# Carrying a small product to its places by transfers, and moving two normalizations to other engines

## The chip, the cores and the metric

The kernel runs on one core of a Trainium2 chip. The metric is the device time of one execution in microseconds (us); lower is better. A core has five engines that run side by side, each with its own queue of instructions that is worked off strictly in order: TensorE (PE in the profile; its weight loads are PEld), VectorE (DVE), ScalarE (ACT), GpSimd (POOL) and SyncE (SP), which here issues the transfers (DMAs) and computes nothing. An instruction that has to wait for a semaphore holds up everything behind it in its engine's queue. TensorE writes its products to PSUM, which VectorE and ScalarE can read and GpSimd can't; everything else lies in SBUF, 128 partitions wide.

## The reference

An attention over a memory of 32 slots for each of 8 batches with 8 heads, followed by a mixture of four expert networks over the 4608 rows that it gives:

```python
a = softmax(phi, axis=seq)                      # per batch, head, memory slot; 576 x 32
k_m = einsum('bhsm,bhsd->bhmd', a, k)           # 32 x 64 per head
v_m = einsum('bhsm,bhsd->bhmd', a, v)
scores = (q @ k_m.T) / sqrt(64)                 # 576 x 32 per head
attn = softmax(scores, axis=-1)
x = (attn @ v_m)  ->  4608 x 512                # all heads side by side
p = domain_probs / sum(domain_probs)
out = sum over e of p[:, e] * (relu(x @ w1[e]) @ w2[e])   # w1 512 x 1024, w2 1024 x 512
```

All inputs and the output are float32.

## The kernel before, in words

**Precision.** TensorE multiplies numbers of a shorter form (F32R). So a float32 operand is split in two parts: ScalarE writes a rounded copy (the high part), and VectorE or GpSimd subtracts it from the original (the remainder, the low part). A product then takes three matmuls: high by high, high by low, low by high. `split` (line 146) does this for a stretch of w1 or w2: line 147 is the copy, line 148 the subtraction.

**The main loop.** The product x @ w1 is never formed through x. Since x = attn @ v_m, the kernel multiplies v_m by w1 once per pair of batches and expert (called vw), and then attn by vw. There are 512 steps, 128 for each of four pairs of batches (`PAIR`), 32 for each expert, 8 for each half of a batch; a step stands for 128 of the 1024 hidden columns and 256 or 320 rows. `steps` (line 838) does four things for step s: `accumulate` of a finished group; `run_plan(s)`; `first(s + 2)`, the product attn @ vw with the relu (lines 554 to 556 on TensorE, line 566 the relu as high part on ScalarE, line 568 its remainder on VectorE); and `second(s)`, the product with w2 (lines 584 to 586). So the relu and the remainder of a step have two steps' time before `second` needs them.

**The plan.** Everything else is put into `plan`, a table written by hand of what is emitted in which step: loads and splits of w1 and w2, the attention of batches 1 to 7, the products vw. For batches 2 to 7 the table `ATT` gives the first step, the step of the write (`written`), the steps of the three score products and of the three transposes. The program is in that order on each engine from step 36 on (`manual_schedule`), and so is the part ahead of step 0, a sequence for batch 0 written out by hand. In steps 0 to 35 a scheduler may move instructions.

**Attention of a batch b that starts at step s.** `load_phi` at s; `phi_max` at s + 3; `phi_exp` at s + 4; `phi_norm` (line 209) at s + 5 and s + 6 for the two halves g: add a small number to the sum, take the reciprocal, multiply phi by it (line 213), and copy its last 64 columns behind it (line 214). Then come transposes on TensorE (line 228) and the products with k and v (line 283), into `v` and `kT` (`kv_pick`, line 306). `scores_mm` multiplies q by k_m, and one step later each, `scores_max` (VectorE), `scores_exp` (ScalarE, line 411) and `soft` follow; the last one ends in a product of the exponentials with the reciprocal of their sum (line 421). `transposes` (line 442) turns the result for `first`.

**Where v_m goes.** `v` of a batch lies on 128 partitions by 4 by 32. Two layouts are made of it. `vts[k]` (line 102) holds both batches of pair k with heads in the slots that `TURN` gives, high and low part side by side; `vw_mm` (line 459) multiplies it by w1, and `vw_out` (line 478) splits the product, a copy by ScalarE (line 482) and a subtraction by VectorE (line 483) for each of the batches asked for. It is written for batches 0 to 3 (`write_vt`). `vs` holds four batches, the high part on the first 64 partitions and the remainder on the other 64; `four` (line 501) multiplies it by w1 for four batches at once, and `to_memory` and `load_vw` take the results through HBM. It is written for all batches (`write_vs`): batches 0 to 3 are first read in step 72, batches 4 to 7 in step 232.

Before, `v_hi` (line 340) makes the high part `vh` on ScalarE (line 347); `write_vt` (line 350) brings the parts to their places by operations on 64 partitions, copies by VectorE where the place lies in the other half of the partitions (line 363), or by ScalarE where it doesn't (line 360), and subtractions by VectorE (line 364); `write_vs` (line 366) does the same with ScalarE (line 376) and VectorE (lines 378, 379). The steps `written` are 48 and 65 for batches 2 and 3, and 163, 181, 195 and 216 for batches 4 to 7; `write_vs` stands one step later.

**Loads.** SyncE issues all transfers. `take` (line 137) hands out a load and issues loads ahead, each of which waits for its stage buffer to be free.

## Time and profile before

| | |
|---|---|
| median of 3 runs | 1428.37 us (1424.88 to 1428.73) |
| profiled execution, whole | 1426.93 us |
| its span, first to last instruction | 1425.1 us |
| granted TensorE clock, mean over the span | 0.995 |
| TensorE busy | 1397.7 us |
| VectorE busy | 663.7 us |
| ScalarE busy | 568.3 us |
| GpSimd busy | 396.0 us |

The profile is of one execution. Its views: busy time of each engine, for the whole span or for stretches of it (a stretch's row gives its length, then for each engine the busy time and in brackets the count of instructions, then the granted clock, the share of time in which the DMA engines were busy, and GB/s); groups of instructions by line and shape (busy time, mean ns of one, and the idle time of the engine just before them with what ended it); waits (who waited for whom: total us, times, longest); the chain of waits that ended last; the timeline (start, length, engine, line, operation, what is written <- what is read, shapes, count, and in square brackets the idle time before it with what ended it); and transfers by line (KB each, median us from issue to landing). Line 12 of the kernel is L12. SPq and ACTq mark what an engine's queue itself does, such as issuing a transfer.

### The profile page before, as it was taken

How to read it: one execution, taken by the hardware profiler on the slowest of the kernel's cores; microseconds unless marked ns; L12 is line 12 of the kernel's file. 1: busy time of each engine (PE TensorE's matmuls, PEld its weight loads, DVE VectorE, ACT ScalarE, POOL GpSimd, SP SyncE). 2: the span in 40 equal slices, each digit the busy share in tenths (PEclk: the TensorE clock that was granted, in tenths of full speed). 3: DMA queues.
4: the chain of work that ended last, by engine and by line, in shares of the span. 5: the costliest groups of instructions: out<-in, count | busy, mean ns of one | idle time of the engine just before them, and what ended most of it. 6: DMA issues, size and time to landing. Idle time of an engine off the chain costs nothing.

```text
span 1425.1 us, 21643 instructions
## 1 busy us (share of the span) xinstructions
PE 1397.7 (98%) x7742; PEld 1218.4 (85%) x7742; DVE 663.7 (47%) x1562; ACT 568.3 (40%) x1524; POOL 396.0 (28%) x316
## 2 busy tenths in 40 slices
PE   7999999999999989999999999999999999999998
PEld 6888888888888878888888888888888888888887
DVE  7986556435553476464343345434343322223222
ACT  7655445433344445453353443534332312122221
POOL 4300244322234244342242433424220202020200
PEclk9999999999999999999999999999999999999999
DMA  6532322585232233245368676786841633233201
GB/s 235 177 106 89 106 94 83 195 251 154 75 122 86 70 130 99 75 134 138 104 234 265 231 265 185 260 229 213 256 141 45 186 75 103 75 104 75 60 30 37
DMA packets 62843, 199.16 MB, mean 140 GB/s; under 512 B 10384, under 2 KB 11536, under 8 KB 62736
## 3 DMA queue, kind: packets, MB, share of 16 engines
q1 hardware_dynamic: 62736, 197.77, 44.0%
q8 instruction: 62, 1.02, 0.3%
q14 instruction: 45, 0.37, 0.1%
HBM read 146.35 MB, written 51.38 MB: 139 GB/s over the span
## 4 chain that ended last, share of the span: by engine, by line
PE 90%; DVE 6%; ACT 2%; issue 1%; DMA 1%; SPq 0%; ACTq 0%; DVEq 0%
PE p L586 18%; PE p L584 17%; PE p L585 17%; PE p L554 9%; PE p L555 9%; PE p L556 9%; PE pv L507 3%; PE sc L392 2%; PE x L283 2%; DVE vw L483 1%; ACT vw L482 1%; PE pv L462 1%; PE pv L464 1%; PE pv L463 1%; DVE vt L364 1%
## 5 line engine op out<-in xcount | busy, mean ns | idle before, releaser
L148 POOL TENSOR_TENSOR w<-stage,w 128x512 fp32r<-128x512 f32 x230 | 297.5, 1297 | 752.7 <-ACT w L147 727.8
L568 DVE SCALAR_TENSOR_TENSOR h<-p,h 128x256 fp32r<-128x256 f32 x512 | 215.2, 421 | 427.0 <-ACT h L566 289.4
L586 PE MATMUL p<-w,h 128*128 128x512 f32 x1024 | 403.1, 394 | 5.6 <-DVE h L568 4.9
L584 PE MATMUL p<-w,h 128*128 128x512 f32 x1024 | 403.7, 394 | 0.0
L585 PE MATMUL p<-w,h 128*128 128x512 f32 x1024 | 403.1, 394 | 0.0
L566 ACT ACTIVATE h<-p 128x256 fp32r<-128x256 f32 x512 | 196.4, 384 | 488.6 <-PE p L556 471.2
L554 PE MATMUL p<-AT,vw 128*128 128x256 f32 (+1 forms) x1024 | 309.1, 302 | 1.9 <-DVE vw L483 1.8
L555 PE MATMUL p<-AT,vw 128*128 128x256 f32 (+1 forms) x1024 | 302.7, 296 | 0.3 <-DVE AT L454 0.3
L556 PE MATMUL p<-AT,vw 128*128 128x256 f32 (+1 forms) x1024 | 301.6, 295 | 0.1
L586 PEld LDWEIGHTS p<-w,h 128*128 128x128 f32 x1024 | 192.8, 188 | 50.4 <-DVE h L568 5.8
L554 PEld LDWEIGHTS p<-AT,vw 128*128 128x128 f32 x1024 | 193.1, 189 | 23.1 <-PE pv L464 2.5
L584 PEld LDWEIGHTS p<-w,h 128*128 128x128 f32 x1024 | 192.7, 188 | 23.3 <-ACT h L566 0.2
L585 PEld LDWEIGHTS p<-w,h 128*128 128x128 f32 x1024 | 192.9, 188 | 22.1
L555 PEld LDWEIGHTS p<-AT,vw 128*128 128x128 f32 x1024 | 193.9, 189 | 20.1 <-DVE AT L454 0.5
L556 PEld LDWEIGHTS p<-AT,vw 128*128 128x128 f32 x1024 | 192.8, 188 | 0.8 <-DVE vw L483 0.7
L147 ACT CAST w<-stage 128x512 fp32r<-128x512 f32 x264 | 162.1, 618 | 5.1 <-DMA stage<-in_w 2.8
L568 DVE SCALAR_TENSOR_TENSOR hm<-p,hm 128x64 fp32r<-128x64 f32 x256 | 56.0, 219 | 148.4 <-ACT h L566 146.8
L566 ACT ACTIVATE hm<-p 128x64 fp32r<-128x64 f32 x256 | 57.1, 223 | 160.4 <-PE p L556 160.4
L510 DVE TENSOR_TENSOR vst<-pv,vst 128x512 fp32r<-128x512 f32 x80 | 55.3, 692 | 113.1 <-ACT vst L509 112.8
L272 POOL TENSOR_TENSOR kvs<-stage,kvs 128x512 fp32r<-128x512 f32 x58 | 74.4, 1302 | 107.4 <-ACT kvs L271 106.5
L509 ACT CAST vst<-pv 128x512 fp32r<-128x512 f32 x80 | 47.0, 587 | 123.4 <-PE pv L507 123.4
L483 DVE TENSOR_TENSOR vw<-pv,vw 64x512 fp32r<-64x512 f32 x96 | 65.7, 687 | 29.8 <-ACT vw L482 28.1
(89 smaller groups left out, 1174.6 us busy)
## 6 DMA issues: line engine op xcount, KB each, us to landing
stage<-in_w SPq DMA_DIRECT2D x92, 512.0 KB, 4.0
vwd<-vst SPq DMA_DIRECT2D x80, 512.0 KB, 3.5
vw<-vwd SPq DMA_DIRECT2D x320, 128.0 KB, 4.1
stage<-in_w1d SPq DMA_DIRECT2D x40, 512.0 KB, 3.8
stage<-in_kv SPq DMA_DIRECT2D x32, 512.0 KB, 3.8
stage<-in_qm SPq DMA_DIRECT2D x16, 512.0 KB, 4.1
out<-acc SPq DMA_DIRECT2D x32, 256.0 KB, 2.1
ph<-in_phi SPq DMA_DIRECT2D x16, 288.0 KB, 4.5
```

Source lines behind the costliest of these rows:

```text
L147: nc.scalar.copy(dst[:, 0, :], raw)
L148: eng.tensor_sub(dst[:, 1, :], raw, dst[:, 0, :].bitcast(F32))
L272: eng.tensor_sub(t[:, 1], src, t[:, 0].bitcast(F32))
L483: nc.vector.tensor_sub(t[r, 1, :], ps[r], t[r, 0, :].bitcast(F32))
L554: nc.tensor.matmul(ps, w[:, 0, f], at_t[:, g, 0, c], start=g == 0, stop=False)
L555: nc.tensor.matmul(ps, w[:, 0, f], at_t[:, g, 1, c], start=False, stop=False)
L556: nc.tensor.matmul(ps, w[:, 1, f], at_t[:, g, 0, c], start=False, stop=g == 1)
L566: nc.scalar.activation(t[:, 0, to], ps[:, at_], AF.Relu)
L568: nc.vector.scalar_tensor_tensor(t[:, 1, to], ps[:, at_], 0.0, t[:, 0, to].bitcast(F32), ALU.max, ALU.subtract)
L584: nc.tensor.matmul(po[t], x[:, 0, :], w[:, 0, :], start=j == 0, stop=False)
L585: nc.tensor.matmul(po[t], x[:, 0, :], w[:, 1, :], start=False, stop=False)
L586: nc.tensor.matmul(po[t], x[:, 1, :], w[:, 0, :], start=False, stop=j == NJ - 1)
```

## The change

Five edits:

- `v_hi`, `write_vt` and `write_vs` are replaced. `v_split` makes both parts of the whole of `v` in two operations, a copy by ScalarE and a subtraction by GpSimd, into one tile `vh` of both parts with a single buffer (before: two buffers of half the size). `write_v` carries the parts to `vs`, and for batches 2 and 3 to `vts` too, by transfers issued by ScalarE: 8 for a batch, 16 where both are written, each of 64 partitions by 64 numbers (16 KB). Batches 0 and 1 keep the operations for `vts` (`write_vt_0`).
- The steps: `v_split` stands where the high part was made, `write_v` one step later. For batches 0 and 1 they move from steps 20 and 21 to 16 and 18, and 22 and 24.
- `phi_norm` for all batches but the first: the product with the reciprocal and the copy move from VectorE to ScalarE.
- `soft` from batch 2 on: the last product moves from VectorE to GpSimd.
- `vw_out` with two batches: first both copies, then both subtractions, where before each copy was followed by its subtraction.

```diff
@@ -210,8 +210,12 @@
         ph, zs = st["ph", b][:, g], st["zs", b, g]
         nc.vector.tensor_scalar_add(zs, zs, 1e-9)
         nc.vector.reciprocal(zs, zs)
-        nc.vector.tensor_scalar_mul(ph[:, :S], ph[:, :S], zs)
-        nc.vector.tensor_copy(ph[:, S:], ph[:, 512:S])
+        if b == 0:
+            nc.vector.tensor_scalar_mul(ph[:, :S], ph[:, :S], zs)
+            nc.vector.tensor_copy(ph[:, S:], ph[:, 512:S])
+        else:
+            nc.scalar.activation(ph[:, :S], ph[:, :S], AF.Copy, scale=zs)
+            nc.scalar.copy(ph[:, S:], ph[:, 512:S])
 
     def phi_chain(b):
         for g in range(2):
@@ -337,46 +341,41 @@
     def slot(b, h):
         return h ^ TURN[b % 4]
 
-    def v_hi(b, gs=slice(0, 2)):
-
-        if ("vh", b) not in st:
-            st["vh", b] = att.tile([P, NP, M], F32R, name="vh", tag="vh", bufs=2)
-        split = lambda t: t.rearrange("p (g a) m -> p g a m", g=2)
-        v, vh = split(st["v", b]), split(st["vh", b])
-        if gs is not None:
-            nc.scalar.copy(vh[:, gs], v[:, gs])
-        return v, vh
-
-    def write_vt(b, gs=slice(0, 2)):
-
-        v, vh = v_hi(b, None)
+    def write_vt_0(b, gs=slice(0, 2)):
+
         vt = vts[b // 2].rearrange("p (g a) s c -> p g a s c", g=2)
+        v = st["v", b].rearrange("p (g a) m -> p g a m", g=2)
         for h in range(4):
             q = slot(b, h)
-            r, rq = (slice(64 * (i % 2), 64 * (i % 2) + 64) for i in (h, q))
+            r = slice(64 * (h % 2), 64 * (h % 2) + 64)
             dst = vt[r, gs, h // 2, :, M * q:M * q + M]
-            x, hi = v[rq, gs, q // 2, :], vh[rq, gs, q // 2, :]
-            if r == rq:
-                nc.scalar.copy(dst[:, :, 0, :], x)
-                hi = dst[:, :, 0, :]
-            else:
-                nc.vector.tensor_copy(dst[:, :, 0, :], hi.bitcast(F32))
-            nc.vector.tensor_sub(dst[:, :, 1, :], x, hi.bitcast(F32))
-
-    def write_vs(b):
+            x = v[r, gs, q // 2, :]
+            nc.scalar.copy(dst[:, :, 0, :], x)
+            nc.vector.tensor_sub(dst[:, :, 1, :], x, dst[:, :, 0, :].bitcast(F32))
+
+    def v_split(b):
+
+        st["vh", b] = att.tile([P, 2, NP, M], F32R, name="vh", tag="vh")
+        split(st["vh", b].rearrange("p s a m -> p s (a m)"),
+              st["v", b].rearrange("p a m -> p (a m)"), nc.gpsimd)
+
+    def write_v(b, pair):
+
 
         if b % 4 == 0:
             st["vs", b // 4] = att.tile([P, 2, 4, P], F32R, name="vs", tag="vs")
-        vs, (v, vh) = st["vs", b // 4], v_hi(b, None)
+        vs = st["vs", b // 4]
+        vt = vts[b // 2].rearrange("p (g a) s c -> p g a s c", g=2) if pair else None
+        v = st["vh", b].rearrange("p s (g a) m -> p s g a m", g=2)
         for h in range(4):
             q = slot(b, h)
             rq, c = slice(64 * (q % 2), 64 * (q % 2) + 64), slice(M * q, M * q + M)
-            x, hi = v[rq, :, q // 2, :], vh[rq, :, q // 2, :]
-            if q % 2 == 0:
-                nc.scalar.copy(vs[:64, :, h, c], hi.bitcast(F32))
-            else:
-                nc.vector.tensor_copy(vs[:64, :, h, c], hi.bitcast(F32))
-            nc.vector.tensor_sub(vs[64:, :, h, c], x, hi.bitcast(F32))
+            rh = slice(64 * (h % 2), 64 * (h % 2) + 64)
+            for i in range(2):
+                src = v[rq, i, :, q // 2, :].bitcast(F32)
+                nc.scalar.dma_start(vs[64 * i:64 * i + 64, :, h, c].bitcast(F32), src)
+                if pair:
+                    nc.scalar.dma_start(vt[rh, :, h // 2, i, c].bitcast(F32), src)
 
     def tiles(t0):
         return (2, P) if t0 < 4 else (1, 64)
@@ -418,7 +417,7 @@
         nc.vector.reduce_sum(zv[:, :, 0], av, AX.X)
         nc.vector.tensor_scalar_add(zv[:, :, 0], zv[:, :, 0], 1e-9)
         nc.vector.reciprocal(zv[:, :, 0], zv[:, :, 0])
-        nc.vector.tensor_mul(av, av, zv.broadcast_to([n, nt * H, M]))
+        (nc.gpsimd if b > 1 else nc.vector).tensor_mul(av, av, zv.broadcast_to([n, nt * H, M]))
 
     def q_key(b, t0):
         return ("qm", b, t0 // 2) if t0 < 4 else ("qt", b)
@@ -476,10 +475,10 @@
         return slice(64 * q, 64 * q + 64)
 
     def vw_out(ps, k, e, fh, hp, odds):
-        for odd in odds:
-            t = vw_tile(k, e, odd, fh, hp // 2)
-            r = vw_rows(2 * k + odd, hp)
+        to = [(vw_tile(k, e, odd, fh, hp // 2), vw_rows(2 * k + odd, hp)) for odd in odds]
+        for t, r in to:
             nc.scalar.copy(t[r, 0, :], ps[r])
+        for t, r in to:
             nc.vector.tensor_sub(t[r, 1, :], ps[r], t[r, 0, :].bitcast(F32))
 
     def vw_unit(k, e, fh, hp, odds, tag):
@@ -617,7 +616,7 @@
         u = [lambda g=g: (phi_turn(b, g), phi_turn_out(b, g)) for g in range(2)]
         u += [lambda: (phi_turn_tail(b), phi_turn_tail_out(b)), unit_tail(b)]
         u += [unit_kv(b, hp) for hp in range(NP)]
-        u += [lambda: write_vt(b)]
+        u += [lambda: write_vt_0(b)]
         u += [unit_scores(b, t0) for t0 in (0, 2, 4)]
         u += [lambda t0=t0: (transposes(b, t0), transposes_out(b, t0)) for t0 in (0, 2, 4)]
         return u
@@ -633,7 +632,8 @@
     for s, u in zip(REST_0, rest):
         at(s, u)
     for b in range(2):
-        at(20 + b, lambda b=b: (v_hi(b), write_vs(b)))
+        at(16 + 6 * b, lambda b=b: v_split(b))
+        at(18 + 6 * b, lambda b=b: write_v(b, False))
 
     at(UNITS_1[0], lambda: phi_chain(1))
     for i, u in enumerate(att_units(1)):
@@ -669,11 +669,8 @@
         for g in range(2):
             at(s + 18 + 6 * g, lambda g=g: [kv_fold(b, 2 * g + i) for i in range(2)])
             at(s + 19 + 6 * g, lambda g=g: kv_pick(b, g))
-        def write():
-            if b < 4:
-                write_vt(b)
-        at(written, lambda: (v_hi(b), write()))
-        at(written + 1, lambda: write_vs(b))
+        at(written, lambda: v_split(b))
+        at(written + 1, lambda: write_v(b, b < 4))
         for t0, n in zip((0, 2, 4), scores):
             at(n, (q_key(b, t0), lambda q, t0=t0: scores_mm(b, t0, q)))
             at(n + 1, lambda t0=t0: scores_max(b, t0))
@@ -803,7 +800,7 @@
         split_w1(w1g[0], 0, 0, gps)
         for hp in (2, 3):
             kv_out(0, hp)
-        write_vt(0, slice(0, 1))
+        write_vt_0(0, slice(0, 1))
         q = raw["qm", 0, 0]
         scores_mm(0, 0, q, (0, 1))
         for hp in (2, 3):
@@ -812,7 +809,7 @@
         kv_pick(0, 1)
         scores_mm(0, 0, q, (2, 3))
         split_w1(w1g[0], 0, 1, gps)
-        write_vt(0, slice(1, 2))
+        write_vt_0(0, slice(1, 2))
         keep_warm(2)
         split_w1(w1g[1], 0, 2, gps)
         split_w1(w1g[1], 0, 3, gps)
```

## The prediction

> **What bounds the kernel now.** I read the totals first, then busy time by stretch, the waits, and the timeline at each stretch where TensorE stands still.
>
> ```profile
> span 1425.1 us, 21643 instructions
> PE 1397.7 (98%) x7742; PEld 1218.4 (85%) x7742; DVE 663.7 (47%) x1562; ACT 568.3 (40%) x1524; POOL 396.0 (28%) x316
> ```
>
> TensorE is busy for 98% of the span, and the change takes no product away from it. So all that can be won is time in which TensorE waits, or runs at a lower granted clock because it had waited. The next view gives both by stretch: length, TensorE's busy time, weight loads, VectorE, ScalarE, GpSimd, granted clock, DMA.
>
> ```profile
> 36.00:160.00 124.00, 121.51 (x695) 103.76 (x696) 94.06 (x217) 69.75 (x170) 20.77 (x16) 1.00 0.39 128
> 160.00:240.00 80.00, 78.39 (x447) 69.14 (x446) 42.51 (x107) 40.14 (x114) 31.84 (x25) 1.00 0.25 80
> 240.00:260.00 20.00, 16.69 (x85) 14.26 (x85) 12.82 (x27) 7.18 (x19) 8.41 (x7) 0.91 0.24 80
> 260.00:490.00 230.00, 229.94 (x1282) 200.92 (x1281) 109.91 (x256) 94.15 (x251) 70.01 (x55) 1.00 0.45 145
> 490.00:536.00 46.00, 40.94 (x228) 34.88 (x227) 31.41 (x56) 22.65 (x52) 18.02 (x14) 0.93 0.32 108
> 536.00:640.00 104.00, 102.13 (x586) 88.87 (x585) 60.59 (x154) 56.13 (x155) 46.15 (x36) 1.00 0.31 99
> 640.00:1425.10 785.10, 781.34 (x4270) 683.11 (x4268) 284.69 (x693) 251.68 (x703) 183.37 (x142) 1.00 0.49 151
> ```
>
> Length minus busy time is what TensorE lost: 2.5 us from 36 to 160, 1.6 to 240, 3.3 to 260, nothing to 490, 5.1 to 536, 1.9 to 640. The clock takes a further 0.09 x 20 = 1.8 us at 240 to 260, and 0.07 x 46 = 3.2 us at 490 to 536. Together 19.4 us: no version of this change can win more. After 640 only the tail is open.
>
> Who is late? In the waits (engine and line, for whom, us in total, times, longest), ScalarE and VectorE hold each other up in vw_out, and TensorE waits for VectorE's normalizations:
>
> ```profile
> ACT vw L482 <- DVE vw L483: 34.0, 34, 3.8
> DVE vw L483 <- ACT vw L482: 28.1, 51, 0.7
> PE tpa L228 <- DVE ph L213: 2.4, 2, 1.6
> PE tp L442 <- DVE at L421: 2.7, 2, 1.9
> ```
>
> **Prices of what moves.** Groups by form: count, busy us, mean ns, idle before.
>
> ```profile
> L213 DVE TENSOR_SCALAR ph<-ph,zs 128x576 f32<-128x576 f32 x16 | 12.4, 778 | 0.5
> L214 DVE COPY ph<-ph 128x64 f32<-128x64 f32 x16 | 5.5, 344 | 0.4
> L206 ACT ACTIVATE ph<-ph,nm 128x576 f32<-128x576 f32 x16 | 12.4, 775 | 8.6 <-DVE nm L200 8.5
> L319 ACT COPY v<-kvp 64x64 f32<-64x64 f32 x32 | 6.6, 207 | 0.9 <-DVE kT L319 0.6
> L421 DVE TENSOR_TENSOR at<-at,z 128x512 f32<-128x512 f32 x16 | 11.2, 703 | 0.4
> L148 POOL TENSOR_TENSOR w<-stage,w 128x512 fp32r<-128x512 f32 x230 | 297.5, 1297 | 752.7 <-ACT w L147 727.8
> ```
>
> Normalizing phi (14 of 16 halves) leaves VectorE, 0.78 + 0.34 us each, and costs ScalarE 0.78 + 0.21 us: 14 us by 14 us. The attention product goes from 0.70 us on VectorE to 1.30 us on GpSimd. The Trainium skill (GPSIMD Engine Reference, Engine selection) sends two-input elementwise work to VectorE, GpSimd being about twice as slow; the two rows agree, and whether that costs time depends on who waits (below).
>
> The transfers are issued by ScalarE: 8 for each of the eight batches, 8 more where vt is written too (batches 2 and 3), 80 in all. No ScalarE issue is in this trace; SyncE's are the nearest rows.
>
> ```profile
> 18.04 0.33 SPq L133 DMA_DIRECT2D stage<-in_w  x1
> 751.98 4.82 SPq L532 DMA_DIRECT2D vw<-vwd x8
> SPq L532 <- DMA stage<-in_w: 6.9, 8, 1.5
> 192.57 1.57 SPq L133 DMA_DIRECT2D stage<-in_kv  x2
> stage<-in_kv SPq DMA_DIRECT2D x32, 512.0 KB, 3.8
> stage<-in_qt SPq DMA_DIRECT2D x8, 128.0 KB, 3.1
> ```
>
> One issue alone holds its queue 0.33 us, eight in a row 0.60 us each, waits included. I take 0.45 us, between them, and keep 0.33 and 0.60 as ends. The Trainium skill (DMA: Bandwidth & Descriptors, Issuing engines are not separate DMA queues) calls the issue time usually small beside the transfer; by that the sum would be the third rival's. The third row says that an issue can also wait for the landing of an earlier transfer that has nothing to do with its data; ScalarE may inherit this.
>
> Costed at nothing: GpSimd's new remainder (128 x 128, a quarter of line 148's elements, so an estimate of 0.3 to 0.4 us, eight times) lies in an engine that is busy for 28% of the span; without that cover it would delay the first transfer of a remainder, and so ScalarE, by one line-148 operation, 1.3 us. The landing itself: the smallest transfer with a row lands after 3.1 us, and the first reader of batch 3's vs is the product of step 72, six steps behind the write; 7.2 + 3.1 = 10.3 us fits in six steps of 2.1 (12.5 us), but not 9.6 + 3.1 = 12.7 us. Batch 0 to 2 have more room. The one vh buffer is free again before the next batch comes, 6 steps later or more. SyncE's next loads may wait for ScalarE's landings, but are issued several steps ahead.
>
> **Part by part.** Batch 3's write (step 65 and 66) is where the clock falls:
>
> ```profile
> 242.53 0.58 ACT L482 CAST vw<-pv 64x512 fp32r<-64x512 f32 x1 [1.96 <-DVE vw L483]
> 243.52 0.28 PE L554 MATMUL p<-AT,vw 128*128 128x256 f32 x1
> 245.61 0.28 PE L554 MATMUL p<-AT,vw 128*128 128x256 f32 x1
> 244.19 1.14 DVE L363 CAST vt<-vh 64x64 fp32r<-64x64 f32 x1
> 249.53 0.21 DVE L364 TENSOR_TENSOR vt<-v,vh 64x64 fp32r<-64x64 f32 x1
> 250.25 0.50 PE L586 MATMUL p<-w,h 128*128 128x512 f32 x1 [3.31 <-DVE h L568]
> 245.07 0.38 ACT L566 ACTIVATE h<-p 128x256 fp32r<-128x256 f32 x1
> ```
>
> Operations of one small shape take 1.1 us or 0.2 us, and VectorE is held from 244.19 to 249.7: TensorE stops for 3.3 us. That goes, and the clock's 1.8 us with it. In its place ScalarE issues 16 transfers, 7.2 us, and behind them in its queue stands the relu of line 566, for which VectorE and then TensorE wait. A relu has two steps before its product is due, 2 x 2.09 us from the two L554 rows, less its own 0.38 us and VectorE's like share: 3.4 us of cover. ScalarE arrives about 1 us sooner, as the 1.96 us wait goes. Stall 7.2 - 1 - 3.4 = 2.8 us plus some 1.8 us of clock: 4.6 for 5.1, **-0.5 us** (ends -4.2 and +1.9).
>
> Batch 2's write (steps 48, 49):
>
> ```profile
> 189.70 0.41 ACT L376 CAST vs<-vh 64x64 fp32r<-64x64 f32 x2
> 195.14 1.20 PE L283 MATMUL x<-kvs,a 128*128 128x256 f32 x8 [1.61 <-DVE a L251]
> 196.29 0.31 PE L554 MATMUL p<-AT,vw 128*128 128x320 f32 x1
> 199.92 0.31 PE L554 MATMUL p<-AT,vw 128*128 128x320 f32 x1
> ```
>
> The 1.6 us stall goes. Steps are 3.6 us here, so the cover is 7.2 - 0.8 = 6.4 us and 16 issues cost 0.8 us. But SyncE's loads of kv at 192.57 stand just before them; if the eighth issue waits for such a landing, 3.8 us later at 196.4, the hold is 6.7 + 8 x 0.45 = 10.3 us, the stall 3.9. I take 2.9, nearer the wait, since the trace shows SyncE waiting so: **+1.3 us** (ends -1.6, +3.5).
>
> 490 to 524: vw_out's chain is copy, remainder, copy, remainder, with ScalarE blocked in the middle of each pair; when VectorE also has a maximum or normalization to do, ScalarE stands for microseconds (the waits row: 3.8 us at the longest). With the copies together ScalarE is held 2 x 0.58 us and leaves; VectorE's two phi normalizations go as well. Of the 8.3 us lost, about 1 us is at the transposes of step 166, next; of 7.3 I count **-6 us** (ends -7.3, -4): what is late next is VectorE's remainders, which stay.
>
> Step 164 to 166, where soft(4, 0) and its transposes are one step apart:
>
> ```profile
> 525.54 0.63 ACT L411 ACTIVATE at<-at 128x512 f32<-128x512 f32 x1
> 526.33 1.14 ACT L271 CAST kvs<-stage 128x512 fp32r<-128x512 f32 x2
> 527.03 2.51 POOL L272 TENSOR_TENSOR kvs<-stage,kvs 128x512 fp32r<-128x512 f32 x2 [0.16 <-ACT kvs L271]
> 531.71 0.69 DVE L421 TENSOR_TENSOR at<-at,z 128x512 f32<-128x512 f32 x1
> ```
>
> Batch 4's 8 transfers stand ahead of this exponential: it ends at 525.5 + 3.6 + 0.6 = 529.7. The casts of kv follow, and GpSimd's two remainders (2.5 us) stand ahead of the product in its queue, which so ends at 529.7 + 0.6 + 2.5 + 1.3 = 534.1, against 532.4 now. TensorE's transposes wait for it, and all of TensorE behind them: 1.7 us and a little clock, **+2 us** (ends +0.9, +3.1, by the issue price).
>
> The rest: 536 to 640, half of 1.9 us goes with phi and the pairs, **-0.8** (-1.2 to +0.5; 8 transfers, 3.6 us, are about the cover). 36 to 160, VectorE is the busiest helper (94 of 124 us) and loses batch 0 and 1's copies and two batches' phi, ScalarE gains 16 issues that the scheduler may place early: **-1.0** (-2 to +2). GpSimd's other products that have one step to spare (steps 104, 114, 173) are the ones with half the elements: half of the two rows' 0.6 us more each, of which I count two of the three, **+0.6** (0.3 to 1).
>
> **Sum:** -0.5 + 1.3 - 6 + 2 - 0.8 - 1.0 + 0.6 = -4.4 us: span 1420.7 us. The profiled execution took 1426.93 us, 1.8 over its span, and lies 1.4 below the median of 1428.37; so 1422.5 on the one, 1424.0 on the other: **1423.5 us**. About 0.3% (4.3 us) is what a measurement here can tell from none.
>
> **Rivals.** *Slower: ScalarE's queue becomes the bound.* If an issue holds ScalarE 0.60 us, 16 hold it 9.6: batch 3 +1.9, batch 2 +3.0, step 166 +3.1, 36 to 160 +2, 536 to 640 +0.5, the other products +0.6, and 490 to 524 gives only -5: +6.1 us, 1434. It decides from about 0.51 us per issue, where the sum crosses zero. For it: the eight in 4.82 us. Against: these include SyncE's waits. *No change:* if the remainders must wait for the second copy of the pair, the reordering moves the wait instead of removing it, 490 to 524 gives -3, step 166 with the slower GpSimd takes 3: about 0, 1428. For it: line 482 waits for line 483 though both only read the product, so whatever couples them stays. *Cheap issues:* 0.33 us, no waiting for landings: batch 2 -1.6, batch 3 -4.2, step 166 +0.9, the others -7, -2, -1.2, +0.3: -14.8, 1413.6.
>
> **Chances.** Forecast 0.40, slower 0.25, no change 0.23, cheap issues 0.12. The forecast's own spread (-9 to 0) puts 0.25 of it beyond 0.3%; with cheap issues and a little of the no-change case faster has 0.40, same 0.34, slower 0.26. The range, 1414 to 1434, reaches from cheap issues to the slower rival.
>
> **What would show it.** Right: line 482 no longer waits for line 483 for tens of us; the clock stays at 1.00 from 490 to 524; TensorE's wait at 246.6 turns into one for ScalarE's line 566, near 250; ScalarE's issues are 0.4 to 0.5 us apart; the transposes' wait (line 442) now names GpSimd. Wrong: issues of 0.6 us with stalls over 5 us at batches 2 and 3, or no stall there at all; or VectorE late again in 490 to 524.

## The result and the profile after

| | before | after |
|---|---|---|
| median | 1427.39 us of 4 runs (1424.88 to 1428.73) | 1440.22 us of 4 runs (1438.17 to 1442.83) |
| ratio after : before | | 1.0093, 95% interval 1.0070 to 1.0116 |
| profiled execution, whole | 1426.93 us | 1440.98 us |
| its span | 1425.1 us | 1439.2 us |

The kernel became 12.8 us slower, 0.9%. The prediction was 1423.5 us, with a range up to 1434: the sign and the range are both wrong. The page's totals after:

```profile
span 1439.2 us, 21661 instructions
PE 1399.6 (97%) x7742; PEld 1221.4 (85%) x7742; DVE 612.7 (43%) x1452; ACT 579.0 (40%) x1536; POOL 417.6 (29%) x342
```

VectorE was relieved of 51 us of work, and TensorE does the same products as before. Its busy time grew by 1.9 us (1397.7 to 1399.6), so 12.2 of the 14.1 us that the span grew are waiting. The view by stretch, with the stretches of the prediction (length, TensorE, weight loads, VectorE, ScalarE, GpSimd, granted clock, DMA), shows where:

```profile
36.00:160.00 124.00, 118.94 (x676) 101.23 (x677) 88.51 (x197) 71.86 (x174) 23.61 (x18) 1.00 0.41 132
160.00:240.00 80.00, 72.96 (x410) 64.56 (x409) 28.74 (x78) 36.10 (x102) 28.47 (x23) 0.96 0.23 70
240.00:260.00 20.00, 18.41 (x106) 15.93 (x104) 9.71 (x20) 9.95 (x24) 8.17 (x7) 1.00 0.37 114
260.00:490.00 230.00, 225.99 (x1247) 197.81 (x1248) 102.20 (x239) 97.27 (x254) 79.85 (x64) 0.99 0.45 146
490.00:536.00 46.00, 45.41 (x264) 39.10 (x263) 23.68 (x49) 24.10 (x56) 15.86 (x13) 1.00 0.24 75
536.00:640.00 104.00, 96.69 (x552) 84.77 (x551) 48.60 (x125) 55.91 (x148) 46.90 (x39) 0.97 0.34 109
640.00:1439.20 799.20, 793.87 (x4338) 693.74 (x4336) 284.31 (x693) 258.13 (x720) 196.86 (x156) 1.00 0.49 150
```

Read TensorE's busy time against the length. From 490 to 536, where 5.1 us had been lost, 0.6 us are lost now: that part of the change works. From 160 to 240 the loss grew from 1.6 to 7.0 us, from 536 to 640 from 1.9 to 7.3 us, and a new 4.0 us stand at the start of 260 to 490. Since stalls shift everything behind them, stretches by the clock on the wall mix places. A cleaner account: TensorE does the same 7742 products in the same order in both kernels (apart from some between 50 and 149 us), so for each product one can say how far one kernel lags behind the other. The growth of this lag from one mark to the next, with the marks in the time of the kernel before (in the other tables below too), worked out from the two traces and rounded (sums are taken before rounding):

| stretch (time before) | what lies there | predicted (ends) | lag grew by |
|---|---|---|---|
| 0 to 36 | ahead of step 0 | not counted | +0.9 |
| 36 to 160 | scheduled steps, batches 0 and 1 | -1.0 (-2 to +2) | +2.0 |
| 160 to 240 | batch 2's write | +1.3 (-1.6 to +3.5) | +7.0 |
| 240 to 300 | batch 3's write | -0.5 (-4.2 to +1.9) | +3.0 |
| 300 to 490 | main loop | 0 | -0.3 |
| 490 to 528 | vw_out with phi | -6 (-7.3 to -4) | -6.3 |
| 528 to 536 | step 166's transposes | +2 (+0.9 to +3.1) | +7.9 |
| 536 to 640 | phi and pairs | -0.8 (-1.2 to +0.5) | 0.0 |
| 640 to the end | | 0 (+0.6 for GpSimd's other products) | 0.0 |
| sum | | -4.4 | +14.0 |

Three places carry the result. In the waits after (engine and line, for whom, us in total, times, longest; line numbers have shifted a little, the relu is at 565 instead of 566, the exponential at 410 instead of 411), the same three places have names:

```profile
DVE vw L482 <- ACT vw L480: 23.3, 34, 1.3
ACT hm L565 <- DMA vt<-vh: 13.5, 1, 13.5
ACT h L565 <- DMA vt<-vh: 10.4, 1, 10.4
ACT at L410 <- issue: 7.5, 1, 7.5
PE pv L461 <- DVE hm L567: 7.0, 1, 7.0
PE tp L441 <- POOL at L420: 6.8, 1, 6.8
PE p L583 <- ACT h L565: 6.2, 2, 5.6
```

The first line is what is left of the two engines holding each other up in vw_out: ScalarE's 34 us of waiting for VectorE are gone. The next three are new: ScalarE's relu stood behind the issuing of transfers for 13.5 us (batch 2) and 10.4 us (batch 3), the exponential of step 164 for 7.5 us. Such a time, in which ScalarE's queue only issues or waits to issue, is called a hold below. "DMA vt<-vh" as releaser means the issuing instruction of that transfer, not its landing. The last three are what TensorE paid: 7.0, 6.8 and 5.6 us, each one step further along the chain. What an issue costs stands in the views of lines 376 and 378 (engine, operation, count: least, median, longest ns):

```profile
L376 ACTq DMA_DIRECT2D vs<-vh x64: 597/617/1359, 35.3 to 705.9; - x64
L378 ACTq DMA_DIRECT2D vt<-vh x16: 597/618/676, 191.3 to 262.9; - x16
```

The shortest of 80 took 0.597 us, against the 0.45 us of the prediction, and in a row they start 0.66 us apart. The timeline of ScalarE at batch 2's write shows a second thing:

```profile
194.66 0.62 ACTq L376 DMA_DIRECT2D vs<-vh  x1
195.35 0.60 ACTq L378 DMA_DIRECT2D vt<-vh  x1
199.57 0.60 ACTq L376 DMA_DIRECT2D vs<-vh  x1
200.21 0.62 ACTq L378 DMA_DIRECT2D vt<-vh  x1
...
205.47 0.62 ACTq L378 DMA_DIRECT2D vt<-vh  x1
206.14 0.22 ACT L565 ACTIVATE hm<-p 128x64 fp32r<-128x64 f32 x1 [13.49 <-DMA vt<-vh]
```

Ten issues back to back from 199.57 on, but a hole of 3.6 us ahead of them. In the trace each transfer has one of eight completion semaphores, which come round in turn for SyncE's and ScalarE's transfers alike; the issue at 199.57 waits for the semaphore of a load of kv:

```profile
195.81 1.57 SPq L133 DMA_DIRECT2D stage<-in_kv  x2
```

The first of the two landed at 199.55. It has nothing to do with v_m's data. At step 164 both things meet again (ScalarE, then GpSimd):

```profile
530.57 0.60 ACTq L376 DMA_DIRECT2D vs<-vh  x1
531.21 7.95 ACTq L376 DMA_DIRECT2D vs<-vh  x7
539.21 0.63 ACT L410 ACTIVATE at<-at 128x512 f32<-128x512 f32 x1 [7.55 <-issue]
```

```profile
540.70 2.49 POOL L276 TENSOR_TENSOR kvs<-stage,kvs 128x512 fp32r<-128x512 f32 x2 [5.78 <-ACT kvs L275]
543.58 1.05 POOL L420 TENSOR_TENSOR at<-at,z 128x512 f32<-128x512 f32 x1 [0.40 <-DVE z L419]
```

Seven issues take 7.95 us, of which 7 x 0.66 = 4.6 are issuing and 3.3 the wait for another kv load (issued 533.60, landed 537.89). The exponential comes at 539.21, GpSimd's remainders and its product behind it, and the transposes start at 544.68.

### The profile page after: what moved, and what is told of

It reads as the page before. It is cut to its first block, busy times and chain, and to the rows that moved or that the text cites. A ratio compares the mean times of both kernels' runs of the same rounds, so it can differ in the third digit from the quotient of the medians.

```text
span 1439.2 us, 21661 instructions
## 1 busy us (share of the span) xinstructions
PE 1399.6 (97%) x7742; PEld 1221.4 (85%) x7742; DVE 612.7 (43%) x1452; ACT 579.0 (40%) x1536; POOL 417.6 (29%) x342
## 4 chain that ended last, share of the span: by engine, by line
PE 61%; ACT 1%; ACTq 0%; POOL 0%; DVE 0%; DMA 0%; issue 0%; POOLq 0%
PE p L585 12%; PE p L583 12%; PE p L584 12%; PE p L553 6%; PE p L554 6%; PE p L555 6%; PE pv L506 2%; PE sc L391 1%; PE x L287 1%; ACTq L376 0%; PE tp L441 0%; DMA stage<-in_kv 0%; PE kvp L306 0%; POOL kvs L276 0%; ACT w L147 0%
## 5 line engine op out<-in xcount | busy, mean ns | idle before, releaser
L482 DVE TENSOR_TENSOR vw<-pv,vw 64x512 fp32r<-64x512 f32 x96 | 66.0, 688 | 24.5 <-ACT vw L480 23.3
```

What stands on the lines that cost most here:

```text
L482: nc.vector.tensor_sub(t[r, 1, :], ps[r], t[r, 0, :].bitcast(F32))
```

## The experiments

The theory after this result: the operations that were moved gain a few us, and the transfers would gain too, but 80 issues of 0.62 us stand in the queue of the engine that feeds TensorE every step; where 8 or 16 stand in a row, with waits for landings of other loads among them, they cost 27 us. Rivals: the transfers themselves (landing, contention) cost it; GpSimd's product costs it at step 166; moving phi costs it. Times are medians; a ratio is to the kernel before in the same runs (1426.5 to 1427.8 us).

**The operations without the transfers.** `v_split`, `write_v` and their steps are taken back to the operations of before; the other three edits stay. The main place:

```diff
-        at(written, lambda: v_split(b))
-        at(written + 1, lambda: write_v(b, b < 4))
+        def write():
+            if b < 4:
+                write_vt(b)
+        at(written, lambda: (v_hi(b), write()))
+        at(written + 1, lambda: write_vs(b))
```

> The changed kernel with the transfers undone: v_m goes to its places by operations as before; phi on ScalarE, the attention product on GpSimd and the copies ahead of the remainders stay. Theory (ScalarE's queue is held by its issues, 0.66 us each, and by landings that they wait for): the three long stalls of the changed kernel (7 us near 200, 6 near 260, 7 near 540) go, the two of the kernel before near 193 and 247 come back (about 2 and 5 us), the gain at 490 to 533 stays: 1418 to 1424 us. Rival (GpSimd's slower product and remainder make the wait at step 166): that wait stays above 5 us, 1426 to 1432 us.

Measured: 1422.16 us, ratio 0.9961 (0.9947 to 0.9976). So the whole loss comes in with the transfers, 18.1 us.

**The same transfers, issued by SyncE.**

```diff
-                nc.scalar.dma_start(vs[64 * i:64 * i + 64, :, h, c].bitcast(F32), src)
+                nc.sync.dma_start(vs[64 * i:64 * i + 64, :, h, c].bitcast(F32), src)
                 if pair:
-                    nc.scalar.dma_start(vt[rh, :, h // 2, i, c].bitcast(F32), src)
+                    nc.sync.dma_start(vt[rh, :, h // 2, i, c].bitcast(F32), src)
```

> The changed kernel with the same transfers issued by SyncE. Theory: ScalarE is free, the three long stalls go and those of the kernel before do not come back: 1413 to 1420 us, with SyncE's issues of these transfers 0.35 to 0.5 us apart. Rival (small transfers are dear on any queue and hold what stands behind them): SyncE needs 0.66 us for each too, its loads come late, ScalarE waits for stage loads by 5 us or more: 1428 us or more.

Measured: 1413.42 us, ratio 0.9903 (0.9888 to 0.9918): 26.8 us less than after, with the same bytes moved by the same transfers. TensorE loses nothing at batches 2 and 3, and 0.5 us from 536 to 640, where it had lost 7.3 (the view by stretch):

```profile
160.00:240.00 80.00, 80.00 (x459) 70.86 (x458) 34.76 (x90) 43.71 (x119) 32.86 (x27) 1.00 0.26 83
240.00:260.00 20.00, 20.00 (x112) 17.54 (x112) 9.16 (x20) 8.55 (x23) 10.24 (x9) 1.00 0.42 129
...
536.00:640.00 104.00, 103.49 (x602) 91.32 (x601) 48.05 (x124) 58.74 (x157) 45.15 (x38) 1.00 0.31 101
```

One part of the expectation fell. The issues are no cheaper on SyncE (view of line 376):

```profile
L376 SPq DMA_DIRECT2D vs<-vh x64: 590/605/704, 30.2 to 675.8; - x64
```

0.6 us is the price of this transfer, not of ScalarE. It is only that behind SyncE's issues nothing stands that TensorE soon waits for. The rule of the Trainium skill that the prediction weighed (DMA: Bandwidth & Descriptors, Issuing engines are not separate DMA queues), that the choice of the issuing engine saves only the sequencer's issue time, agrees with this pair. That this time is usually small does not hold here: 0.6 us of issue stand beside 1.9 to 2.1 us from issue to landing, and whose queue pays them was worth 1.9%.

**The same issues by ScalarE, spread.** From batch 2 on one head per step, over four steps (`write_v` takes the heads as one more argument).

```diff
-        at(written + 1, lambda: write_v(b, b < 4))
+        for h in range(4):
+            at(written + 1 + h, lambda h=h: write_v(b, b < 4, (h,)))
```

> The changed kernel with a batch's transfers (from batch 2 on) spread over four steps, one head in each: 2 or 4 issues at a time, still by ScalarE, as many in all. Theory (what costs is that 8 or 16 issues in a row outlast the two steps of cover): holds of 1.3 and 2.6 us are hidden, the stalls near 200 and 260 go or fall below 2 us: 1416 to 1424 us. Rival (every issue costs its 0.66 us wherever it stands, 80 of them): no change, 1436 to 1442 us. Rival (the data land late): worse than 1440 us.

Measured: 1415.24 us, ratio 0.9915 (0.9898 to 0.9931), a little under what was expected. ScalarE still issues all 80 in the same queue as the relu, at the same price, yet next to nothing is lost (views of line 376 and by stretch):

```profile
L376 ACTq DMA_DIRECT2D vs<-vh x64: 597/610/1665, 35.7 to 681.8; - x64
```

```profile
160.00:240.00 80.00, 78.92 (x451) 69.66 (x450) 33.26 (x86) 42.05 (x116) 32.36 (x26) 1.00 0.27 83
240.00:260.00 20.00, 20.00 (x112) 17.59 (x111) 9.42 (x23) 9.48 (x25) 9.42 (x8) 1.00 0.33 93
```

So it is not the 80 issues but their standing in one piece that costs: a step of batches 2 and 3 absorbs four of them, 2.6 us.

**Batch 2's transfers seven steps later,** away from the loads of kv.

```diff
-        at(written + 1, lambda: write_v(b, b < 4))
+        at(written + (8 if b == 2 else 1), lambda: write_v(b, b < 4))
```

> The kernel after, with one line changed: batch 2's sixteen transfers are issued by ScalarE in step 56 (the step of its split plus 8) instead of step 49, away from SyncE's kv loads at 193 to 196 us. Theory (the hold of 13.5 us at batch 2 is 16 issues of 0.65 us, 10.4 us, plus a 3.1 us wait for the landing of a load that has nothing to do with them): the gap between two issues is gone, ScalarE is held 10 to 11 us in one run of issues, TensorE's stall there falls from 8.9 to 5 to 6.5 us, and the time is 1435.5 to 1438.5 us. Rival (the gap is a fixed price of sixteen issues in a row, or of the queue's depth, wherever they stand): the gap returns at the new place, hold 13 to 14 us, stall 8 to 9 us, 1439.5 to 1441.5 us.

Measured: 1437.61 us, ratio 1.0070 (1.0055 to 1.0085), 2.6 us under after, though the two intervals overlap. ScalarE's timeline has no hole any more:

```profile
213.64 0.60 ACTq L376 DMA_DIRECT2D vs<-vh  x1
214.26 0.65 ACTq L378 DMA_DIRECT2D vt<-vh  x1
...
223.50 0.62 ACTq L378 DMA_DIRECT2D vt<-vh  x1
224.24 0.38 ACT L565 ACTIVATE h<-p 128x256 fp32r<-128x256 f32 x1 [10.24 <-DMA vt<-vh]
```

Sixteen issues in 10.5 us, and the lag at batch 2 grows by 3.6 us instead of 7.0. The difference, 3.4 us, is about the hole of 3.6. So the price of the issues and the wait for an unrelated landing are told apart. Against the same transfers issued by SyncE, where the lag shrinks by 2.0 us here, batch 2 cost 9.0 us: 3.4 for the landing and 5.6 for the issues.

**Batches 4 to 7 issued by SyncE, 0 to 3 by ScalarE.**

```diff
+        q_dma = nc.sync if b >= 4 else nc.scalar
         for h in range(4):
...
-                nc.scalar.dma_start(vs[64 * i:64 * i + 64, :, h, c].bitcast(F32), src)
+                q_dma.dma_start(vs[64 * i:64 * i + 64, :, h, c].bitcast(F32), src)
...
```

> The kernel after, with the transfers of batches 4 to 7 (32 of 80) issued by SyncE, those of batches 0 to 3 still by ScalarE. Theory (each hold of ScalarE has a price of its own, and the prices add up): the 9.0 us lost at the transposes of step 166 fall to 1 to 2 us and the 0.9 us at 640 goes, batch 2's 8.9 and batch 3's 8.1 us stay; 1430.5 to 1433.5 us. Rival (a stall at 537 to 548 is there anyway, because GpSimd's remainders of kv and its product stand in one queue, and the issues only come on top): 3 us or more stay lost at 537 to 548, 1433.5 to 1437 us.

Measured: 1430.67 us, ratio 1.0024 (1.0014 to 1.0034). The lag at step 166 falls from +7.9 to -0.2, at 536 to 640 from 0.0 to -2.0, while batches 2 and 3 keep theirs (+6.9 and +2.8). The prices are local and add up, and with GpSimd's product alone TensorE's transposes wait 0.6 us at step 166.

**Attention's product on VectorE again.**

```diff
-        (nc.gpsimd if b > 1 else nc.vector).tensor_mul(av, av, zv.broadcast_to([n, nt * H, M]))
+        nc.vector.tensor_mul(av, av, zv.broadcast_to([n, nt * H, M]))
```

> The changed kernel with the attention product back on VectorE for all batches. Theory: the stall at step 166 is ScalarE's hold ahead of the exponential; the product's engine is worth 1 to 3 us there: 1436 to 1439 us, stall of line 441 still over 4 us. Rival (GpSimd's queue makes that stall): it falls below 2 us, 1431 to 1433 us.

Measured: 1440.67 us, ratio 1.0092 (1.0077 to 1.0107), no different from after. Transposes still wait 6.9 us, now with VectorE's name:

```profile
PE tp L441 <- DVE at L420: 8.7, 2, 6.9
```

The name in a wait is the last link of a chain; the engine named need not be the cause. The small gain that was expected did not come.

**Each transfer into vs as two of half the size.** The suspected cost is raised and the bytes are kept: 144 issues instead of 80.

```diff
-                nc.scalar.dma_start(vs[64 * i:64 * i + 64, :, h, c].bitcast(F32), src)
+                for g in range(2):
+                    nc.scalar.dma_start(vs[64 * i:64 * i + 64, g, h, c].bitcast(F32), src[:, g])
```

> The kernel after, with each of the 64 transfers into vs issued as two of half the size (64 partitions, one run each): 144 issues by ScalarE instead of 80, 24 at batch 2 and 3, 16 at batch 4, the bytes as before. Theory (an issue has a fixed price of about 0.62 us, spent at the rate of 0.65 us, whatever the transfer moves): the halves take 0.58 to 0.62 us each, ScalarE is held 5.2 us longer in each of the three places, TensorE's stalls grow by as much, and the time is 1455 to 1464 us. Rival (the price goes with the number of runs, or descriptors, of the transfer): the halves take 0.30 to 0.45 us each, the holds and stalls stay within 1.5 us, 1440 to 1446 us.

Measured: 1476.58 us, ratio 1.0353 (1.0332 to 1.0373). The halves cost about as much each as the whole ones (0.607 us at the median, 0.468 at the least):

```profile
L377 ACTq DMA_DIRECT2D vs<-vh x128: 468/607/1197, 35.2 to 737.7; - x128
```

The lag grows by 4.9, 4.4 and 5.1 us more than after at batch 2, batch 3 and step 166, close to the 5.2 us expected: the price is per issue. The sum exceeds the expectation because more places appear, at the writes of batches 5 to 7, where eight issues in a row had cost little and sixteen cost more than their cover: there the lag grows by another 20 us. The waits of TensorE name them:

```profile
PE p L584 <- ACT h L566: 19.5, 4, 10.9
PE pv L462 <- DVE hm L568: 12.0, 1, 12.0
PE tp L442 <- POOL at L421: 11.4, 1, 11.4
PE tpa L232 <- ACT ph L217: 6.3, 1, 6.3
```

**Parts of the change alone.** First only the copies ahead of the remainders, on the kernel before:

```diff
-        for odd in odds:
-            t = vw_tile(k, e, odd, fh, hp // 2)
-            r = vw_rows(2 * k + odd, hp)
+        to = [(vw_tile(k, e, odd, fh, hp // 2), vw_rows(2 * k + odd, hp)) for odd in odds]
+        for t, r in to:
             nc.scalar.copy(t[r, 0, :], ps[r])
+        for t, r in to:
             nc.vector.tensor_sub(t[r, 1, :], ps[r], t[r, 0, :].bitcast(F32))
```

> The kernel before, with one part of the change: in vw_out the copies of a pair ahead of its remainders. Theory (it is the half-way block of ScalarE in vw_out that puts VectorE and ScalarE out of step between 490 and 524): most of that stretch's loss goes, ScalarE's wait for line 483 (34 us before) falls under 10 us, and the time is 1422 to 1425 us, 0.2 to 0.4 percent under the kernel before. Rival (the remainders only start later, since they wait for the second copy): the wait moves to VectorE, 490 to 536 stays at 40.5 to 41.5 us of TensorE, 1426 to 1429 us.

Measured: 1415.46 us, ratio 0.9921 (0.9904 to 0.9937), about three times the gain expected. The rows by stretch show that it gains at batch 3's write too, which this edit doesn't touch:

```profile
240.00:260.00 20.00, 19.05 (x106) 16.14 (x105) 14.18 (x34) 8.48 (x23) 9.01 (x7) 1.00 0.32 99
490.00:536.00 46.00, 43.83 (x271) 38.31 (x269) 35.53 (x71) 25.53 (x62) 20.71 (x17) 1.00 0.40 131
```

Why there? GpSimd's timeline in the kernel before, and then in this one:

```profile
243.98 5.01 POOL L148 TENSOR_TENSOR w<-stage,w 128x512 fp32r<-128x512 f32 x4 [2.64 <-ACT w L147]
```

```profile
244.18 1.29 POOL L148 TENSOR_TENSOR w<-stage,w 128x512 fp32r<-128x512 f32 x1 [0.86 <-ACT w L147]
246.20 1.28 POOL L148 TENSOR_TENSOR w<-stage,w 128x512 fp32r<-128x512 f32 x1 [0.74 <-ACT w L147]
248.29 1.29 POOL L148 TENSOR_TENSOR w<-stage,w 128x512 fp32r<-128x512 f32 x1 [0.80 <-ACT w L147]
```

VectorE's four slow small operations of the prediction's rows (1.14, 1.37, 1.18, 1.33 us from 244.19 to 249.07) stand one to one beside GpSimd's four back-to-back remainders, and the fast ones (0.19 to 0.22 us) come right after the last of them. In this kernel ScalarE, which is no longer held in vw_out, hands GpSimd its work in even portions, and VectorE's small operations run in the holes: only one is slow (1.3 us) for each of GpSimd's. The Trainium skill (SBUF — State Buffer, Who interferes with whom) says that a VectorE instruction with two SBUF inputs, or a copy in a two-port mode, and a GpSimd instruction that reads SBUF block each other for a whole instruction; the slow subtractions, which read v and vh from SBUF, agree, and in which mode the copies ran no row shows. The coincidence in time is shown; that it is the port was not tried by itself.

Then phi on ScalarE alone, and with the copies (the lines for every batch but the first, as in the change):

```diff
+            nc.scalar.activation(ph[:, :S], ph[:, :S], AF.Copy, scale=zs)
+            nc.scalar.copy(ph[:, S:], ph[:, 512:S])
```

> The kernel before, with one part of the change: ScalarE normalizes phi (14 of 16 halves). Theory (VectorE is the late one only where vw_out and phi meet; ScalarE takes 14 us for 14 us): the two waits of the phi transposes (2.4 us) go, a part of 490 to 524 goes, 1424 to 1427 us. Rival (ScalarE, blocked in vw_out, now normalizes late, and TensorE's phi transposes wait for it): these waits grow to 3 us or more, 1428 to 1431 us.

Measured: 1429.18 us, ratio 1.0011 (1.0001 to 1.0021) over ten runs (1426.23 to 1431.56): no gain, and by the 0.3% of the prediction no difference either. The time lies in the rival's range, but the phi transposes wait 1.9 us for ScalarE where they had waited 2.4 us for VectorE: these waits neither went nor grew. By place, in the profiled execution (1430.39 us), the lag shrinks by 3.4 us at 490 to 528, and grows by 1.1 ahead of step 0, by 2.6 from 36 to 160, by 2.7 at step 166 and by 0.6 from there to 640.

> The kernel before, with two parts of the change: copies ahead of remainders, and ScalarE normalizes phi. With attention by GpSimd as well the time was 1422.16 us, with the copies alone 1415.46. Theory (phi on ScalarE is what costs: batch 1's normalization delays the phi transposes at 50 to 70 us, where the three-part kernel loses 5.2 us and the copies alone some 2.8, and again at 508 to 516): 1418 to 1421 us, and the loss at 50 to 70 us is 4.5 to 5.5 us. Rival (attention by GpSimd is what costs, at the transposes of step 166): 1415 to 1417 us.

Measured: 1420.52 us, ratio 0.9954 (0.9941 to 0.9966), 5.1 us over the copies alone. The row by stretch has the place that the theory named:

```profile
36.00:160.00 124.00, 118.13 (x668) 100.00 (x669) 92.96 (x207) 71.94 (x175) 21.58 (x16) 1.00 0.36 126
```

5.9 us are lost there, against 3.3 with the copies alone. Beside the copies, phi on ScalarE is a loss, in this execution most of it from 36 to 160 (with GpSimd's product added, the loss there was 4.6 us: that stretch varies from kernel to kernel).

**Which version is best?** Copies ahead of the remainders and transfers issued by SyncE; phi and attention stay on VectorE (the edits of the kernels above, put together).

> The kernel after, with only two parts of the change left: copies ahead of remainders, and v_m's transfers, here issued by SyncE; VectorE normalizes phi and attention. Theory (the parts add up: transfers issued by SyncE were worth 8.7 us over the same operations without transfers, 1422.16 to 1413.42, of which 4 to 6 us are the stalls at batch 2 and 3 and at step 166; copies alone are at 1415.46): 1409 to 1413 us, the fastest here. Rival (the transfers only took up what phi on ScalarE and attention on GpSimd had cost, so nothing is left to win over the copies alone): 1414 to 1417 us.

Measured: 1411.03 us, ratio 0.9890 (0.9876 to 0.9903), the fastest of all. From 160 to 260 nothing is lost, and 0.2 us from 490 to 536:

```profile
160.00:240.00 80.00, 80.00 (x458) 70.81 (x457) 36.24 (x95) 41.91 (x115) 32.89 (x27) 1.00 0.25 83
240.00:260.00 20.00, 20.00 (x112) 17.54 (x112) 9.15 (x20) 8.55 (x23) 10.22 (x9) 1.00 0.41 130
...
490.00:536.00 46.00, 45.81 (x281) 40.37 (x280) 32.12 (x68) 26.22 (x64) 22.63 (x18) 1.00 0.43 139
```

The same with phi on ScalarE from batch 2 on (`if b <= 1:` in place of `if b == 0:`):

> The kernel after, transfers issued by SyncE, attention by VectorE, and phi normalized by VectorE for batches 0 and 1, by ScalarE from batch 2 on. Theory (phi on ScalarE costs only where batch 1's stands in a full ScalarE queue, at 50 to 70 us; from batch 2 on it is free or a small gain): within 1 us of the kernel in which VectorE normalizes every phi, 1409 to 1413 us. Rival (phi on ScalarE costs at 508 to 516 us too, since the phi transposes of batch 4 wait for it): 1 to 3 us above that kernel.

Measured: 1412.63 us, ratio 0.9902 (0.9887 to 0.9917). The two intervals overlap: whether phi of the later batches costs anything in the whole is not settled. At one place it does: from 490 to 528 the lag shrinks by 7.4 and 7.5 us in the two kernels with the copies first and phi on VectorE, and by 6.3 or 6.4 in every one with the copies first and the later phi on ScalarE, this one included. Ahead of step 0, which these edits hardly touch, the kernels differ by up to 2.2 us, more than that. That batch 1's phi costs is what the runs leave as the likeliest, not shown by itself.

## Why the prediction was wrong

The lag by place, in us, for the kernels that carry the argument (the last row is the sum, and the whole-span difference of the profiled execution to that before):

| place | after | operations only | SyncE issues | copies alone | best |
|---|---|---|---|---|---|
| 0 to 36 | +0.9 | +0.6 | +0.1 | +0.8 | +0.6 |
| 36 to 160 | +2.0 | +2.1 | +2.1 | +0.2 | +1.5 |
| batch 2's write | +7.0 | -0.1 | -2.0 | -0.1 | -1.9 |
| batch 3's write | +3.0 | -3.6 | -5.2 | -3.6 | -5.2 |
| 300 to 490 | -0.3 | -0.3 | -0.3 | -0.3 | -0.3 |
| 490 to 528 | -6.3 | -6.3 | -6.3 | -7.5 | -7.4 |
| step 166 | +7.9 | +3.0 | -0.2 | +1.2 | -1.0 |
| 536 to 640 | 0.0 | -1.5 | -2.0 | -2.0 | -2.0 |
| sum | +14.0 | -6.1 | -13.8 | -11.4 | -15.7 |

**The step that failed** is "I take 0.45 us, between them", the price of one issue. It is 0.62 us, at a rate of 0.66 us. The two rows at hand were of other transfers, both from HBM: 0.33 us for a load of 512 KB, and 0.60 us each for eight loads of 128 KB, "waits included". Taking waits off the second was right, as the view of its line in the kernel before shows (least, median, longest ns):

```profile
L532 SPq DMA_DIRECT2D vw<-vwd x320: 302/419/1824, 292.6 to 1342.9; - x160
```

Eight at the median of 0.42 us are 3.4 of those 4.82 us; the rest is longer issues, gaps and waits, 0.6 us of it a wait for a landing. So 0.45 us was a fair reading of that row. What failed was to carry it over to transfers from SBUF to SBUF, of which the trace had none, and which turned out dearer to issue. Why they are dearer stays open; half the size did not make them cheaper. The prediction put the point from which the slower rival decides at 0.51 us per issue, which mixes in the rival's other terms; by the price alone the forecast's sum crosses zero near 0.58 us (an estimate: its three terms grow by some 35 us for each us of price). The measured price lies beyond both: the rival named *ScalarE's queue becomes the bound* is what happened. That its 0.60 us came so near was luck, since it was a price of 0.42 us with waits in it, and its sum of +6.1 is still less than half of +14.0.

**The model behind the price was right in the main.** Batch 3 by the prediction's own formula, hold - 1 - 3.4 + 1.8 of clock, with the measured hold of 10.4 us: 7.8 us; lost were 5.1 + 3.0 = 8.1. Batch 2, hold - 6.4, with 13.5 us: 7.1 us, and TensorE waited 7.0. Step 164: the prediction moved the product by the hold of 3.6 us and had 1.7 us of stall; with the measured hold, 530.57 to 539.21 = 8.6 us, it is 1.7 + 5.0 = 6.7, and TensorE waited 6.8. So queue, cover and who waits for whom were sound. Put into the prediction's own terms, 0.66 us in place of 0.45 gives +2.9 at batch 3, about +3.5 at batch 2 and +3.7 at step 166, and a sum near +3 instead of -4.4 (an estimate): the price of one issue carried the sign, but not the size. The rest of the +14.0 is mainly in the next two points and in the steps up to 160.

**The wait for an unrelated landing** was foreseen at batch 2 (10.3 - 7.2 = 3.1 us of wait weighed, of which 2.1 us of stall were taken; 3.6 happened, and the run with the later step confirms it), but not counted at step 164, where it was 3.3 us of the 8.6.

**The clock after a stall** was counted in full at batch 3 alone, and as "a little" at step 166. The products behind every long stall start slowly: in the kernel after, the granted clock is 0.59 from 206 to 212 (behind the wait of 7.0 us), 0.58 from 264 to 270 (behind 5.6 us) and 0.60 from 544.6 to 550 (behind 6.8 us), and 1.00 in the next five us each time. By that a stall costs about 2 us more than its wait (an estimate: 0.4 of some 5 us of products). At step 166 the 6.8 us of wait, less the 0.8 us that was there before, are 6.0 of a lag of 7.9.

**490 to 524** was right in size, -6.3 for -6, and right that ScalarE's half-way block was the cause: the copies alone take 7.5 us away there. It was wrong that phi adds to it. Alone, phi on ScalarE takes 3.4 us away there; but beside the copies, which already take 7.5, it gives 1.1 back and 6.3 are left. The two gains are largely the same time.

**Batch 3's old stall** was read as the work of v_m's operations, which go with the transfers ("That goes"). The copies alone take away 3.6 of its 5.1 us while those operations stay: most of them were fast once GpSimd's work left holes. The transfers issued by SyncE take away the rest (-5.2).

**36 to 160** was given as -1.0 with an end at +2; it is +2.0 here, between +1.0 and +4.0 in all kernels with batch 1's phi on ScalarE, and between +0.2 and +1.5 in the three without. The scheduler may place instructions anew there, and this is where the range was least founded. **GpSimd's product** took 1.05 us on the mean, not the 1.30 that was assumed. It was priced at +0.6 elsewhere, of which nothing is to be seen, and as a part of the +2 at step 166. With ScalarE late it costs nothing there (1440.67 without it against 1440.22); where ScalarE isn't late it does: step 166 has +3.0 with it (operations only) and +1.1 without (copies and phi), a term of 1.9 us that only shows once the larger one is gone. Beside SyncE's issues it is 0.8 us (-0.2 with it, -1.0 in the best kernel).

**The other rivals** fell. *Cheap issues* needed 0.33 us. *No change* had the remainders wait for the second copy: VectorE waits 23.3 us for ScalarE there, 28.1 before, and the stretch gained all the same.

**In sum,** by the medians: copies ahead -11.6 (1427.07 to 1415.46), phi +5.1 (to 1420.52), attention +1.6 (to 1422.16; other runs, and the intervals overlap), carrying v_m by transfers -8.7 (to 1413.42), issuing them from ScalarE's queue in one piece +26.8 (to 1440.22). Together +13.2, where +12.8 was measured. Two of the ideas are worth 20 us, and the choice of the queue cost more than both.

## What to carry to other kernels

Before transfers are issued from an engine that computes, multiply their number in one place by the issue price of a transfer of the same kind (if the trace has none of that kind, measure one first) and compare it with the time until that engine's next result is due; a step here took four issues (2.6 us) unnoticed, and not sixteen. Few issues per step, or a queue behind which nothing is due soon, turned the same transfers from a loss of 18 us into a gain of 7 to 9 (against 1422.16, the operations without them). And measure the parts of a change alone: the one reordering of two loops was worth more than the rest together, and part of it was won in a place that it doesn't touch, where another engine's work came more evenly after it.

## What the runs showed of the hardware that was not expected

- An issue of 16 KB (64 partitions, two runs of 128 B each) takes 0.62 us on ScalarE's queue and 0.61 us on SyncE's, one of 8 KB (one run) 0.61 us, a load of 512 KB from HBM 0.33 us and one of 128 KB 0.42 us: here the smallest transfers, from SBUF to SBUF, are the dearest to issue, and halving them makes them hardly cheaper. Which property of them sets the price no run separates.
- Transfers of both queues share eight completion semaphores in this kernel, so an issue on ScalarE's queue stood 3.6 us for a load issued by SyncE.
- After TensorE had stood still for 5.6 to 7.0 us, its granted clock was 0.58 to 0.60 for the next 5 to 6 us, then 1.00 again.
- VectorE's operations on 64 x 64 numbers took 0.2 us, and 1.1 to 1.4 us while GpSimd's remainders ran without a pause.
